# Key tiles transposed without regrouping and read by TensorE with a 16-byte step; wo loaded in three pieces

## The chip, the cores and the metric

The kernel runs on one core of a Trainium2 chip. The metric is device time in microseconds (us) of one launch; medians of all runs of a kernel are quoted. Times of the profile count from the start of the span of one profiled execution, which is one to three microseconds shorter than the time of that run.

## The reference

One decode step: attention with a sliding window over a key and value cache, a GELU layer beside it, and a sigmoid gate that mixes the two. Cut to what matters:

```python
# x: (1,1,576)  k_cache, v_cache: (1,16,32768,128)  wq: (576,4096)  wo: (4096,576)   all bf16
W = 4096                                    # the last 4096 keys of each of 16 heads
q = (x @ wq).reshape(1, 1, 32, 128)...      # 32 query heads, 2 for each key head
scores = einsum("bhqd,bhkd->bhqk", q, k) * 128 ** -0.5
a = (softmax(scores) @ v).reshape(1, 1, 4096) @ wo
b = gelu(x @ w1 + b1) @ w2 + b2
out = g * a + (1 - g) * b                   # g = sigmoid(sum(x * gate_w))
```

Keys and values are 16.8 MB each; all inputs read are 53.6 MB.

## The kernel before

The keys come from memory with the head dimension along the free axis, but TensorE must contract over it, so every key tile is transposed by VectorE in blocks of 32 by 32 words. A word is a pair of bf16 values (`bitcast(FP32)`). A key tile `k_t` holds four heads (HB = 4): partition 4k+b holds rows of head b. After the 32x32 transposes the 32 words of a block would lie in the order (k, b), the four heads interleaved. The kernel before writes them as (b, k) instead, so that the words of one head lie together.

```python
    s_ps = ps_s.tile([P, NCK * 8], FP32, name="s_ps")
    k_cuts = ((32, 32, 64), (64, 64), (64, 64), (64, 32, 32))
    for g in range(NG):                                  # 4 groups of 4 heads
        k_t = big.tile([P, NCK, Dh], BF16, name="k_t", tag="CDBA"[g])
        load(k_t, A_k_cache, g, k_cuts[g])
        for f in range(2):
            kt = kt_pool.tile([P, SL * Dh], BF16, name="kt", tag="kt")     # two buffers
            for u in range(2):
                ...
                nc.vector.transpose(
                    out=kt[:, u * half : (u + 1) * half].bitcast(FP32)
                    .rearrange("p (n b k) -> p n k b", b=HB, k=8),         # regrouped
                    in_=k_t[...].bitcast(FP32)
                    .rearrange("p (n k b) -> p n k b", b=HB, k=8))
            kv = kt[:].rearrange("p (c e b k t) -> p c e b k t", e=2, b=HB, k=8, t=2)
            for b in range(HB):
                for j in range(4):
                    nc.tensor.matmul(                                      # 128 in all
                        s_ps[:, f * 512 : (f + 1) * 512].rearrange("p (c k) -> p c k", k=8),
                        lhsT=qz[:, HB * g + b, j, :],
                        rhs=kv[:, :, j // 2, b, :, j % 2], ...)            # 4-byte step
```

Then come the softmax, the first half of w2, the value matmuls, and wo and the second half of w2 at the end. Large tiles share four buffers by tags: the w2 half takes the buffer of the third key tile ("B"), the four value tiles take C, D, A and C again, wo takes D. All large loads are issued in program order from one DMA queue, so a load that waits for its buffer holds up those behind it.

Of the kernel before, what the change touches and what calls it, by code (L numbers as in the profile page):

```python
# [8 lines left out]
FP32 = mybir.dt.float32  # L9
# [7 lines left out]
def kernel(  # L17
# [21 lines left out]
    HB = 4  # L39
# [3 lines left out]
    SL = NCK // 2  # L43
# [53 lines left out]
    for t in range(2):  # L97
        nc.vector.tensor_copy(
            out=alt[:, t : NI + 1 : 2], in_=par[:, t : t + 1].to_broadcast([P, (NI + 1) // 2])
# [6 lines left out]
    for i in range(NI):  # L106
# [3 lines left out]
            rhs=one_b[0:1, 0:1],  # L110
# [5 lines left out]
    for t in range(2):  # L116
        nc.vector.tensor_tensor(
            out=x2[:, :, t], in0=xs_ps[:], in1=alt[:, t : t + NI], op=ALU.mult
# [13 lines left out]
        out=pen[:], in0=pen[:], scalar1=1e30, scalar2=-1e30, op0=ALU.mult, op1=ALU.add  # L132
# [3 lines left out]
    for j in range(4):  # L136
# [6 lines left out]
        out=junk_row,  # L143
# [17 lines left out]
        out=omg[:], in0=g_t[:], scalar1=-1.0, scalar2=1.0, op0=ALU.mult, op1=ALU.add  # L161
# [3 lines left out]
        out=b2g[:], in0=b2_row, scalar1=omg[0:1, 0:1], scalar2=None, op0=ALU.mult  # L165
# [3 lines left out]
        out=gh[:, 0, :], in0=hi4[:], scalar1=g_t[:, 0:1], scalar2=None, op0=ALU.mult  # L169
# [21 lines left out]
    for j in range(NJ):  # L191
# [3 lines left out]
            rhs=ident[0:2, 0:2],  # L195
# [6 lines left out]
    for i in range(NI):  # L202
        for j in range(NJ):
# [3 lines left out]
                rhs=x2[:, i, :],  # L207
# [11 lines left out]
        out=poly[:],  # L219
# [20 lines left out]
    for i in range(NI):  # L240
        for j in range(Hq // 2):
# [3 lines left out]
                rhs=x2[:, i, :],  # L245
# [7 lines left out]
    for j in range(4):  # L253
# [3 lines left out]
            rhs=q_b[:],  # L257
# [3 lines left out]
    for b in range(4):  # L261
# [4 lines left out]
            out=diag[:, :, 0:512].rearrange("p h (j m) -> p h j m", m=P)[:, :, :, 0:2],  # L266
            in_=qj_ps[quad].rearrange("p j h t -> p h j t"),
# [8 lines left out]
    def load(tile_, cache, g, cuts):  # L276
        src = head_rows(cache, g)
        c0 = 0
        for n in cuts:
            nc.sync.dma_start(  # L280
                out=tile_[:, c0 : c0 + n, :].rearrange("p c d -> p (c d)"),
                in_=src[:, :, c0 * Dh : (c0 + n) * Dh],
            )
            c0 += n
# [3 lines left out]
    for g in range(NG):  # L288
# [3 lines that stand above are left out]
            kt = kt_pool.tile([P, SL * Dh], BF16, name="kt", tag="kt")  # L292
            for u in range(2):
                half = SL * Dh // 2
                c0 = f * SL + u * SL // 2
                nc.vector.transpose(  # L296
                    out=kt[:, u * half : (u + 1) * half]
                    .bitcast(FP32)
                    .rearrange("p (n b k) -> p n k b", b=HB, k=8),
                    in_=k_t[:, c0 : c0 + SL // 2, :]  # L300
                    .rearrange("p c d -> p (c d)")
                    .bitcast(FP32)
                    .rearrange("p (n k b) -> p n k b", b=HB, k=8),
                )
            kv = kt[:].rearrange("p (c e b k t) -> p c e b k t", e=2, b=HB, k=8, t=2)
            for b in range(HB):
                for j in range(4):
                    h = HB * g + b
                    nc.tensor.matmul(  # L309
                        s_ps[:, f * 512 : (f + 1) * 512].rearrange("p (c k) -> p c k", k=8),  # L310
                        lhsT=qz[:, h, j, :],
                        rhs=kv[:, :, j // 2, b, :, j % 2],
                        start=(h == 0 and j == 0),
                        stop=(h == Hkv - 1 and j == 3),
                        skip_group_check=True,
                    )
# [10 lines left out]
        out=mh4[:],  # L327
# [11 lines left out]
        out=negm[:], in0=pen[:], in1=mb_ps[:].to_broadcast([P, HB]), op=ALU.add  # L339
# [4 lines left out]
    for f in range(2):  # L344
        cs = slice(f * SL, (f + 1) * SL)
        for b in range(HB):
            nc.scalar.activation(  # L347
                out=p_t[:, cs, :, b],
                in_=s_ps[:, f * 512 : (f + 1) * 512].rearrange("p (c k) -> p c k", k=8),
# [6 lines left out]
            out=pt[:, cs, :].rearrange("p c h -> p (c h)"),  # L356
            in_=p_t[:, cs, :, :].rearrange("p c k b -> p (c k b)"),
# [6 lines left out]
    for f in range(NJ):  # L364
# [13 lines left out]
        out=rgh[:],  # L378
# [8 lines left out]
    for g in range(NG):  # L387
        v_t = big.tile([P, NCK, Dh], BF16, name="v_t", tag="CDAC"[g])
        load(v_t, A_v_cache, g, v_cuts[g])
        for c in range(NCK):  # L390
# [3 lines left out]
                rhs=pt[:, c, 8 * g : 8 * g + 8],  # L394
# [5 lines left out]
    RO = Hq * Dh // P  # L400
    wo_t = big.tile([P, RO, D], BF16, name="wo_t", tag="D")
    wo_src = A_wo.rearrange("(p r) n -> p r n", r=RO)
    for r0, r1 in ((0, 12), (12, RO)):
        nc.sync.dma_start(out=wo_t[:, r0:r1, :], in_=wo_src[:, r0:r1, :])
    for j0, j1 in ((0, 9), (9, 14), (14, 16), (16, 17), (17, 18)):
        nc.sync.dma_start(out=w2_t[:, NJ + j0 : NJ + j1, :], in_=w2_src[:, 1, j0:j1, :])
# [3 lines left out]
        out=om[:], in0=o_ps[:].to_broadcast([P, Hq, 4]), in1=rgh[:], op=ALU.mult  # L410
# [10 lines left out]
    for f in range(NJ, NF):  # L421
# [5 lines left out]
        out=out.rearrange("a b (s d) -> (a b s) d", s=2), in_=out_row[0:64:32, :]  # L427
# [31 lines left out]
```

## Time and profile before

| | before |
|---|---|
| median time | 150.57 us (3 runs, 149.56 to 151.6) |
| profiled span | 149.5 us |
| key transposes, VectorE | 16 of 3776 ns, 30.7 to 89.0 us |
| score matmuls, TensorE | 128 of 512 columns; 216 ns apart at best |
| scores end | 94.4 us |
| DMA | 53.8 MB, two holes |

The page shows the span in 40 slices of 3.7 us; a digit is a busy share in tenths (slices are counted from 0 below), PEclk is the clock granted to TensorE. These are four rows of part 2 of the page of the kernel before, and the two lines of part 4, the chain of work that ended last:

```profile
PE   0189991700768188909094949550069936361791
DVE  5990022099999999999999980406350000100001
PEclk9999999999999956999969595997555555555579
DMA  5999999999999999950089999999963899999940
...
DVE 38%; DMA 33%; PE 15%; ACT 7%; issue 5%; SPq 0%; DVEq 0%; ACTq 0%
DVE kt L296 34%; DMA wo_t<-in_A_wo_dram 14%; DMA wq_t<-in_A_wq_dram 14%; ACT p_t L347 6%; PE y_ps L178 5%; PE o_ps L391 5%; DMA w_t<-in_B_w_dram 4%; PE s_ps L309 4%; DVE pt L355 2%; DVE m L320 1%; PE q_ps L242 1%; PE t_ps L373 0%; DVE qz_flat L265 0%; DVE out_row L425 0%; PE mt_ps L322 0%
```

VectorE is busy without a gap from slice 8 to slice 23. The DMA row has a hole at slices 18 and 19 (67 to 75 us) and a dip at 29 and 30 (108 to 116 us). The chain says the same: the transposes of line 296 are its largest part.

The groups of the same page, with busy time and mean ns after the bar, and idle time before them after the second bar:

```profile
L296 DVE STREAM_TRANSPOSE kt<-k_t 128x2048 f32<-128x2048 f32 x16 | 58.3, 3776 | 0.0
L309 PE MATMUL s_ps<-kt,qz_flat 128*128 128x512 bf16 x128 | 38.6, 466 | 26.1 <-DVE kt L296 26.1
```

VectorE waits for nothing; TensorE waits 26.1 us for transposes. In the timeline of the key stage (start, length, engine) one sees the batches of 16 matmuls, and the issue of the w2 half on the DMA queue:

```profile
45.57 3.62 PE L309 MATMUL s_ps<-kt,qz_flat 128*128 128x512 bf16 x16 [2.06 <-DVE kt L296]
52.82 6.51 PE L309 MATMUL s_ps<-kt,qz_flat 128*128 128x512 bf16 x16 [3.63 <-DVE kt L296]
74.56 0.34 SPq L363 DMA_DIRECT2D w_t<-in_B_w_dram  x1
89.09 5.30 PE L309 MATMUL s_ps<-kt,qz_flat 128*128 128x512 bf16 x16 [1.95 <-DVE kt L296]
```

A batch takes 3.62 us when the clock is granted in full, which is 216 ns per matmul once the 376 ns of the last one are taken off ((3.62 - 0.376) / 15), and more when the clock is throttled (6.51 us at a mean granted clock of 0.55). The first batch (38.2 us) is an exception: it takes 5.29 us although the record has a full clock there. The Trainium skill ("TensorE: Matmul & The Clock Gate", "Back-to-back issue gap") gives 512/2.4 + 2.5 = 216 ns for a matmul of 512 columns on a warm array; the trace agrees. The section calls this the gap of an isolated matmul and puts a sustained stream at about 131 ns; no batch here averaged less than 215 ns. So with a 4-byte step TensorE reads at its full rate of one column per 0.42 ns.

### The profile page before, as it was taken

To read this page: it belongs to the slowest core of one execution; us is meant where nothing else is said; L and a number is where in the kernel's file an instruction comes from. 1 tells how busy PE (TensorE), PEld (TensorE's weight loads), DVE (VectorE), ACT (ScalarE), POOL (GpSimd) and SP (SyncE) were. 2 spreads that over 40 slices of the span, in tenths; PEclk is the share of its full clock that TensorE was granted. 3 is DMA by queue.
4 is the path that set the end of the run, shared out by engine and by line. 5 is a ranking of instruction groups with operands and counts; after the bars stand their busy time and mean duration, and the time that the engine had idled before them with its cause. 6 is when DMAs were issued, how large, how long until landed. Compare 5 with 4: busy or idle time off the path is not lost.

```text
span 149.5 us, 2460 instructions
## 1 busy us (share of the span) xinstructions
PE 85.1 (57%) x1126; PEld 53.3 (36%) x1126; DVE 78.7 (53%) x81; ACT 11.9 (8%) x21; POOL 0.7 (0%) x6
## 2 busy tenths in 40 slices
PE   0189991700768188909094949550069936361791
PEld 0187991600223022404031313230069936330450
DVE  5990022099999999999999980406350000100001
ACT  3000000010000000000000000099600000000000
POOL 1000000000000000000000000000000000000000
PEclk9999999999999956999969595997555555555579
DMA  5999999999999999950089999999963899999940
GB/s 163 428 429 420 434 431 397 421 445 434 425 421 419 421 434 425 408 237 0 0 277 427 444 438 447 438 460 421 430 298 66 377 403 428 451 437 393 404 158 0
DMA packets 4344, 53.78 MB, mean 360 GB/s; under 512 B 487, under 2 KB 748, under 8 KB 1006
## 3 DMA queue, kind: packets, MB, share of 16 engines
q1 hardware_dynamic: 4324, 53.61, 85.9%
q8 instruction: 9, 0.15, 0.4%
q10 hardware_dynamic: 10, 0.01, 0.0%
q14 instruction: 1, 0.01, 0.0%
HBM read 53.62 MB, written 0.00 MB: 359 GB/s over the span
## 4 chain that ended last, share of the span: by engine, by line
DVE 38%; DMA 33%; PE 15%; ACT 7%; issue 5%; SPq 0%; DVEq 0%; ACTq 0%
DVE kt L296 34%; DMA wo_t<-in_A_wo_dram 14%; DMA wq_t<-in_A_wq_dram 14%; ACT p_t L347 6%; PE y_ps L178 5%; PE o_ps L391 5%; DMA w_t<-in_B_w_dram 4%; PE s_ps L309 4%; DVE pt L355 2%; DVE m L320 1%; PE q_ps L242 1%; PE t_ps L373 0%; DVE qz_flat L265 0%; DVE out_row L425 0%; PE mt_ps L322 0%
## 5 line engine op out<-in xcount | busy, mean ns | idle before, releaser
L296 DVE STREAM_TRANSPOSE kt<-k_t 128x2048 f32<-128x2048 f32 x16 | 58.3, 3776 | 0.0
L309 PE MATMUL s_ps<-kt,qz_flat 128*128 128x512 bf16 x128 | 38.6, 466 | 26.1 <-DVE kt L296 26.1
L309 PEld LDWEIGHTS <-qz_flat 128*128 128x128 bf16 x128 | 14.5, 113 | 49.8 <-issue 39.9
L391 PE MATMUL o_ps<-pt,v_t 128*128 128x8 bf16 x512 | 14.3, 168 | 4.6 <-issue 4.1
L391 PEld LDWEIGHTS <-v_t 128*128 128x128 bf16 x512 | 14.2, 104 | 4.8 <-issue 4.2
L347 ACT ACTIVATE p_t<-s_ps,negm 128x512 bf16<-128x512 f32 x8 | 9.7, 1425 | 66.4 <-DVE negm L338 66.4
L178 PE MATMUL y_ps<-wo_t,ov 128*1 128x288 bf16 x64 | 8.0, 443 | 6.3 <-DMA wo_t<-in_A_wo_dram 6.3
L204 PEld LDWEIGHTS <-w_t 128*128 128x128 bf16 x162 | 10.2, 165 | 1.0 <-issue 1.0
L204 PE MATMUL h_ps<-x,w_t 128*128 128x2 bf16 x162 | 10.4, 202 | 0.0
L409 DVE TENSOR_TENSOR om<-o_ps,rgh 128x128 bf16<-128x128 f32 x1 | 0.3, 291 | 18.0 <-PE o_ps L391 18.0
L425 DVE CAST out_row<-y_ps 33x288 bf16<-33x288 f32 x1 | 0.4, 449 | 16.4 <-PE y_ps L178 16.4
L355 DVE STREAM_TRANSPOSE pt<-p_t 128x2048 bf16<-128x2048 bf16 x2 | 4.6, 2311 | 7.4 <-ACT p_t L347 7.4
L178 PEld LDWEIGHTS <-ov 128*1 128x1 bf16 x64 | 4.0, 122 | 9.9 <-issue 6.3
L373 PE MATMUL t_ps<-ls,ones 128*128 128x32 f32 x2 | 0.6, 398 | 10.8 <-DVE ls L371 10.8
L242 PE MATMUL q_ps<-x,wq_t 128*128 128x2 bf16 x144 | 4.3, 166 | 4.0 <-DMA wq_t<-in_A_wq_dram 4.0
L242 PEld LDWEIGHTS <-wq_t 128*128 128x128 bf16 x144 | 4.1, 104 | 4.2 <-DMA wq_t<-in_A_wq_dram 4.2
L178 PE MATMUL y_ps<-w_t,gt 128*1 128x288 bf16 x72 | 5.3, 289 | 0.0
L213 DVE COPY hacc<-h_ps 128x36 f32<-128x36 f32 x1 | 0.2, 195 | 9.7 <-PE h_ps L204 9.7
L107 PE MATMUL xs_ps<-one_b,rows 1*128 1x1 bf16 x9 | 0.7, 195 | 6.6 <-DVE rows L104 6.6
L373 PEld LDWEIGHTS t_ps<-ls,ones 128*128 128x128 f32 x2 | 0.5, 313 | 11.1 <-issue 11.1
L320 DVE TENSOR_REDUCE m<-s_ps 128x1 f32<-128x1024 f32 x1 | 1.2, 1225 | 5.4 <-PE s_ps L309 5.4
L201 DVE MEMSET qz_flat<- 128x4240 f32 x1 | 3.6, 3592 | 0.9 <-issue 0.9
(66 smaller groups left out, 27.6 us busy)
## 6 DMA issues: line engine op xcount, KB each, us to landing
k_t<-in_A_k_cache_dram SPq DMA_DIRECT2D x6, 2048.0 KB, 31.9
v_t<-in_A_v_cache_dram SPq DMA_DIRECT2D x3, 4096.0 KB, 24.4
w_t<-in_B_w_dram SPq DMA_DIRECT2D x3, 1728.0 KB, 10.4
k_t<-in_A_k_cache_dram SPq DMA_DIRECT2D x4, 1024.0 KB
wo_t<-in_A_wo_dram SPq DMA_DIRECT2D x1, 2880.0 KB
w_t<-in_B_w_dram SPq DMA_DIRECT2D x1, 2592.0 KB
wq_t<-in_A_wq_dram SPq DMA_DIRECT2D x1, 2048.0 KB
v_t<-in_A_v_cache_dram SPq DMA_DIRECT2D x1, 2048.0 KB
```

The lines of the kernel that those rows point to most:

```text
L107: nc.tensor.matmul(xs_ps[:, i : i + 1], lhsT=xdup[:, i : 2 * D : NI], rhs=one_b[0:1, 0:1], start=(i == 0), stop=(i == NI - 1), skip_group_ ...
L178: nc.tensor.matmul(y_ps[32 * s : 32 * s + 1, :], lhsT=vec, rhs=row[:, s * DH : (s + 1) * DH], start=start, stop=stop, skip_group_check=True,)
L201: nc.vector.memset(qz_flat[:].bitcast(FP32), 0.0)
L204: nc.tensor.matmul(h_ps[:, j:NF:NJ], lhsT=w1_t[:, i, j:FH:NJ], rhs=x2[:, i, :], start=False, stop=(i == NI - 1 and j == NJ - 1), skip_grou ...
L242: nc.tensor.matmul(q_ps[:, j : Hq : Hq // 2], lhsT=wq_t[:, i, j * Dh : (j + 1) * Dh], rhs=x2[:, i, :], start=(i == 0 and j == 0), stop=(i ...
L296: nc.vector.transpose(out=kt[:, u * half : (u + 1) * half] .bitcast(FP32) .rearrange("p (n b k) -> p n k b", b=HB, k=8), in_=k_t[:, c0 : c ...
L309: nc.tensor.matmul(s_ps[:, f * 512 : (f + 1) * 512].rearrange("p (c k) -> p c k", k=8), lhsT=qz[:, h, j, :], rhs=kv[:, :, j // 2, b, :, j ...
L320: nc.vector.reduce_max(out=m1[:], in_=s_ps[:], axis=AX.X)
L347: nc.scalar.activation(out=p_t[:, cs, :, b], in_=s_ps[:, f * 512 : (f + 1) * 512].rearrange("p (c k) -> p c k", k=8), func=ACT.Exp, bias=n ...
L355: nc.vector.transpose(out=pt[:, cs, :].rearrange("p c h -> p (c h)"), in_=p_t[:, cs, :, :].rearrange("p c k b -> p (c k b)"),)
L373: nc.tensor.matmul(t_ps[:], lhsT=ones[:], rhs=ls[:], start=True, stop=True)
L391: nc.tensor.matmul(o_ps[:, 8 * g : 8 * g + 8, 0], lhsT=v_t[:, c, :], rhs=pt[:, c, 8 * g : 8 * g + 8], start=(c == 0), stop=(c == NCK - 1),)
```

## The change

The intent: VectorE bounds the key stage, and the regrouping makes its transposes slow, since every word is written 32 bytes from the one before. So transpose plainly, let the four heads stay interleaved, and let TensorE pick every fourth key, which lies 16 bytes from the one before. In addition wo is loaded in three pieces, so that the last matmuls start in smaller batches.

```diff
                 nc.vector.transpose(
-                    out=kt[:, u * half : (u + 1) * half]
-                    .bitcast(FP32)
-                    .rearrange("p (n b k) -> p n k b", b=HB, k=8),
-                    in_=k_t[:, c0 : c0 + SL // 2, :]
-                    .rearrange("p c d -> p (c d)")
-                    .bitcast(FP32)
-                    .rearrange("p (n k b) -> p n k b", b=HB, k=8),
+                    out=kt[:, u * half : (u + 1) * half].bitcast(FP32),
+                    in_=k_t[:, c0 : c0 + SL // 2, :].rearrange("p c d -> p (c d)").bitcast(FP32),
                 )
-            kv = kt[:].rearrange("p (c e b k t) -> p c e b k t", e=2, b=HB, k=8, t=2)
+            kv = kt[:].rearrange("p (c e k b t) -> p c e k b t", e=2, b=HB, k=8, t=2)
...
-                        rhs=kv[:, :, j // 2, b, :, j % 2],
+                        rhs=kv[:, :, j // 2, :, b, j % 2],
...
-    for r0, r1 in ((0, 12), (12, RO)):
+    for r0, r1 in ((0, 12), (12, 24), (24, RO)):
```

## The prediction

> **What bounds it now.** The page puts 34% of the last chain on the key transposes and 33% on DMA. In the timeline 16 transposes run back to back from 30.7 to 89.0 us (3776 ns each, about 3.64 us start to start); the last 16 score matmuls end at 94.4. The DMA queue moves 53.8 MB at about 430 GB/s (some 125 us) and has two holes in the 40 slices: 66-76 us, where the w2 half waits for the third key tile's buffer (issued 74.6), and 109-116 us, where the last value load waits for the softmax and the first 128 value matmuls. The second follows the scores' end by a fixed path (94.4 to 110.3, 16 us).
>
> **What the change does.**
> 1. Transposes lose the regrouping, which writes every word 32 bytes from the last. The contiguous 128x2048 bf16 transpose of this trace takes 2311 ns; I take the same for fp32. VectorE: 58 to 36 us, DMA-paced (1 MiB per 2.45 us): done near 71 us if nothing blocks.
> 2. The 128 score matmuls now read one key per 16 bytes instead of four. Today's 4-byte step runs at full rate: 16 matmuls in 3.62 us at granted clock 1.0, 216 ns apart. The Trainium skill ("SBUF — State Buffer", "Door 1", on cachelines) says that SBUF has 16-byte lines and that full bandwidth needs two hits per line. This trace agrees for other reads: weight loads with a 36-byte step are 63.6 ns apart (54 in 3.43 us), contiguous ones 29.4 ns; VectorE's 128x128 reduction takes 371 ns at a 32-byte step, 266 ns at 8. No moving operand with such a step is in the trace, so its size is an estimate. Most likely half rate: about 427 ns each, 6.9 us per 16, against 4.9 us of key arrival.
> 3. wo in three pieces: the 40 matmuls (4.96 us) that start at 139.1 after the second piece become 24 earlier and 16 later; worth at most 1 us.
>
> **Critical path.** At half rate TensorE replaces VectorE as the limit of the key stage: from 35 us, 8 times 6.9, scores end near 90.5 instead of 94.4. Transposes then wait for kt. The first DMA hole shrinks (w2 issued near 67.5); the second, which counts, ends 4 us earlier. Span about 149.5 - 4 - 0.5 to 1 = 145 us.
> If strided streaming cost nothing or up to 1.5x, scores end at 76-80 us, both holes close, DMA is continuous and the time is about 133-134 us. If it costs four times (850 ns per matmul or more), the key stage takes 110 us and the whole about 200.
> Chances: half rate 0.5, cheap 0.17, about four times 0.33.
>
> **Predicted** 145.5 us, 8 in 10 within 133 to 200. Faster by over 2%: 0.62; within 2%: 0.06; slower by over 2%: 0.32.
>
> **What would show it.** The groups: transpose mean near 2.2-2.3 us; score matmuls about 430 ns apart even at clock 1.0. The waits: TensorE waits for transposes little, VectorE for kt held by matmuls much. The chain: score matmuls in place of transposes. The slices: first hole 2 us or less; second still there. Timeline: last wo batch of 16 matmuls, not 40.
>
> **What would make it wrong.** The one number I can't read: the cost of a 16-byte step on the moving side. Also: fp32 transposes slower than bf16 ones even when contiguous; a lower granted clock when TensorE is busy without gaps.

## The result, and the profile after

The changed kernel takes 202.78 us (median of 4 runs, 202.46 to 203.81) against 150.12 us (4 runs). The ratio is 1.350, with a 95% interval of 1.338 to 1.361: slower by 35%.

The same rows and lines of the page of the changed kernel (a slice is now 5.0 us; the matmul that was line 309 is line 304):

```profile
PE   0599460999999999999999999999973089446563
DVE  6920309441704406208026044000033520000000
PEclk9999999999999999999999999999999555555978
DMA  6999999999999000000999995970000007999980
...
PE 61%; DMA 27%; ACT 5%; DVE 3%; SPq 1%; issue 0%; ACTq 0%
PE s_ps L304 55%; DMA w_t<-in_B_w_dram 15%; DMA k_t<-in_A_k_cache_dram 12%; ACT p_t L342 5%; PE o_ps L386 3%; PE y_ps L178 2%; DVE kt L296 1%; DVE pt L350 1%; DVE m L315 1%; SPq L399 1%; SPq L280 0%; PE t_ps L368 0%; PE mt_ps L317 0%; PE mb_ps L329 0%; DVE out_row L420 0%
...
L304 PE MATMUL s_ps<-kt,qz_flat 128*128 128x512 bf16 x128 | 110.0, 1036 | 5.8 <-DVE kt L296 5.8
L296 DVE STREAM_TRANSPOSE kt<-k_t 128x2048 f32<-128x2048 f32 x16 | 36.2, 2293 | 55.8 <-PE s_ps L304 53.0
```

TensorE is now the row without gaps, from slice 7 to slice 28, and its score matmuls have taken the place of VectorE's transposes in the chain (55%, where those had 34%). The transposes fell from 3776 to 2293 ns, as intended, but they now wait 53.0 us for the matmuls to free kt buffers. The 128 matmuls take 110.0 us. The timeline shows their spacing in the weight loads between them, one for each matmul (the first rows of the stage, then a transpose pair and the issue of the w2 half):

```profile
35.52 110.03 PE L304 MATMUL s_ps<-kt,qz_flat 128*128 128x512 bf16 x128 [5.76 <-DVE kt L296]
36.37 0.13 PEld L304 LDWEIGHTS <-qz_flat 128*128 128x128 bf16 x1 [0.73 <-issue]
37.23 0.12 PEld L304 LDWEIGHTS <-qz_flat 128*128 128x128 bf16 x1 [0.73 <-issue]
38.08 0.12 PEld L304 LDWEIGHTS <-qz_flat 128*128 128x128 bf16 x1 [0.73 <-issue]
...
63.19 4.50 DVE L296 STREAM_TRANSPOSE kt<-k_t 128x2048 f32<-128x2048 f32 x2 [9.23 <-PE s_ps L304]
95.19 0.34 SPq L358 DMA_DIRECT2D w_t<-in_B_w_dram  x1
```

Each matmul takes 0.858 us, over the whole stage 110.03 / 128 = 0.860 us. The granted clock was 1.0 meanwhile, as a window of the stage shows (busy time and number of matmuls, granted clock, DMA):

```profile
core 0: us, PE busy (x), PEclk, DMA share, GB/s
35.50:145.00 109.50, 109.47 (x128) 1.00 0.61 255
```

So the throttle has no part in the loss. The spacing is 1.68 ns per column, four times the 0.42 ns of before. The w2 half is issued at 95.2 us instead of 74.6, because the buffer of the third key tile is freed later, so the first DMA hole grew from two slices of 3.7 us to six of 5.0 us. But that hole isn't what costs the time. The end of the scores moved from 94.4 to 145.6 us, by 51.2 us; the span grew by 51.5 us. What follows the scores takes what it took: 149.5 - 94.4 = 55.1 us before, 201.0 - 145.6 = 55.4 us after.

### The profile page after: what moved, and what is told of

Read it like the earlier page. It is cut to its first block, busy times and chain, and to the rows that moved or that the text cites. A ratio compares the mean times of both kernels' runs of the same rounds, so it can differ in the third digit from the quotient of the medians.

```text
span 201.0 us, 2461 instructions
## 1 busy us (share of the span) xinstructions
PE 158.6 (79%) x1126; PEld 55.6 (28%) x1126; DVE 56.5 (28%) x81; ACT 11.9 (6%) x21; POOL 0.7 (0%) x6
## 4 chain that ended last, share of the span: by engine, by line
PE 61%; DMA 27%; ACT 5%; DVE 3%; SPq 1%; issue 0%; ACTq 0%
PE s_ps L304 55%; DMA w_t<-in_B_w_dram 15%; DMA k_t<-in_A_k_cache_dram 12%; ACT p_t L342 5%; PE o_ps L386 3%; PE y_ps L178 2%; DVE kt L296 1%; DVE pt L350 1%; DVE m L315 1%; SPq L399 1%; SPq L280 0%; PE t_ps L368 0%; PE mt_ps L317 0%; PE mb_ps L329 0%; DVE out_row L420 0%
## 5 line engine op out<-in xcount | busy, mean ns | idle before, releaser
L304 PE MATMUL s_ps<-kt,qz_flat 128*128 128x512 bf16 x128 | 110.0, 1036 | 5.8 <-DVE kt L296 5.8
L296 DVE STREAM_TRANSPOSE kt<-k_t 128x2048 f32<-128x2048 f32 x16 | 36.2, 2293 | 55.8 <-PE s_ps L304 53.0
L304 PEld LDWEIGHTS <-qz_flat 128*128 128x128 bf16 x128 | 15.9, 124 | 98.2 <-issue 96.8
L178 PE MATMUL y_ps<-w_t,gt 128*1 128x288 bf16 x72 | 9.2, 419 | 2.0 <-DMA w_t<-in_B_w_dram 2.0
L178 PE MATMUL y_ps<-wo_t,ov 128*1 128x288 bf16 x64 | 5.8, 343 | 3.4 <-DMA wo_t<-in_A_wo_dram 3.4
L178 PEld LDWEIGHTS <-gt 128*1 128x1 bf16 x72 | 4.5, 116 | 5.5 <-issue 2.2
L178 PEld LDWEIGHTS <-ov 128*1 128x1 bf16 x64 | 3.3, 97 | 5.7 <-issue 3.5
```

Of the source, the lines that this page charges most:

```text
L178: nc.tensor.matmul(y_ps[32 * s : 32 * s + 1, :], lhsT=vec, rhs=row[:, s * DH : (s + 1) * DH], start=start, stop=stop, skip_group_check=True,)
L296: nc.vector.transpose(out=kt[:, u * half : (u + 1) * half].bitcast(FP32), in_=k_t[:, c0 : c0 + SL // 2, :].rearrange("p c d -> p (c d)").b ...
L304: nc.tensor.matmul(s_ps[:, f * 512 : (f + 1) * 512].rearrange("p (c k) -> p c k", k=8), lhsT=qz[:, h, j, :], rhs=kv[:, :, j // 2, :, b, j ...
```

## The experiments

Theory A: the whole loss is the 16-byte step of TensorE's moving operand, and its cost is a fixed time for every 16-byte line of SBUF that the reads touch, about 1.67 ns. Theory B: the step is not the cause; the plain transposes, or the order of the kt buffers between the engines, hold TensorE up. Within A the form of the cost is open: the Trainium skill ("SBUF — State Buffer", "Door 1", the paragraph on cachelines) has a threshold, two hits per line, and then full bandwidth.

Four of the kernels below (e2, e3, e5, e6) read wrong keys. The comparison with the reference doesn't tell whether the right keys were read in this problem. For the variants of which it is said below that they are right, the index map of the regrouped transposes was enumerated apart from the chip, for groups of one, two and four heads, and every value that TensorE reads was found to be the one wanted (no run shows this). For the kernel with quarter transfers (e7) the order was only reasoned out.

### wo in three pieces, alone (e1_wo3)

```diff
-    for r0, r1 in ((0, 12), (12, RO)):
+    for r0, r1 in ((0, 12), (12, 24), (24, RO)):
```

> The kernel before with wo in three pieces alone. Both theories: 0 to 1 us faster (at most the second wo batch of 40 matmuls, 4.96 us, is split into 24 and 16; the last w2 bytes land soon after). If it is slower, part of the loss after the change belongs to wo and not to the key stage.

Measured: 149.71 us against 149.56 us, ratio 1.001 (0.996 to 1.006), 6 and 11 runs. No gain can be seen. In the profile read first the last wo batch is down to 16 matmuls, 1.14 us; in the second one the last two pieces run as one batch of 40 again (4.76 us). In both the end then waits for the last pieces of w2.

### Plain transposes, 4-byte reads (e2_plain_read4)

```diff
-            kv = kt[:].rearrange("p (c e k b t) -> p c e k b t", e=2, b=HB, k=8, t=2)
+            kv = kt[:].rearrange("p (c e b k t) -> p c e b k t", e=2, b=HB, k=8, t=2)
...
-                        rhs=kv[:, :, j // 2, :, b, j % 2],
+                        rhs=kv[:, :, j // 2, b, :, j % 2],
```

(against the changed kernel)

> Plain transposes and wo in three pieces as in the changed kernel, but TensorE keeps its 4-byte step and so reads other words of the same kt buffers: results wrong on purpose. Theory A (the 16-byte step of the moving reads is the whole loss): matmuls 216 ns apart at granted clock 1.0, transposes 2.29 us, scores end near 76 us, both DMA holes closed, 133 to 136 us. Theory B (the plain transposes or the order of the kt buffers hold TensorE up): stays far above 150 us.

Measured: 135.76 us, ratio 0.909 (0.905 to 0.913). The DMA row of its page and three lines of its timeline (second profile):

```profile
DMA  4999999999999999999999998999899999999960
...
62.15 0.33 SPq L358 DMA_DIRECT2D w_t<-in_B_w_dram  x1
67.10 3.62 PE L304 MATMUL s_ps<-kt,qz_flat 128*128 128x512 bf16 x16 [1.30 <-DVE kt L296]
71.48 3.62 PE L304 MATMUL s_ps<-kt,qz_flat 128*128 128x512 bf16 x16 [0.77 <-DVE kt L296]
```

The record's class for this comparison is "unclear"; but the five runs lie between 135.59 and 137.34 us, and none of the kernel before is under 148.75 us. With nothing but the step put back, the same instructions on the same tiles take 3.62 us per batch in seven of the eight batches (5.29 us in the first, as before), the scores end at 75.1 us, and DMA has no hole. Theory B falls for the plain transposes. This is also what the idea would have given, 9%, had the 16-byte step been free; the prediction's 133 to 134 us for that case was close.

### Regrouped transposes, 16-byte reads (e3_regroup_read16)

```diff
-            kv = kt[:].rearrange("p (c e b k t) -> p c e b k t", e=2, b=HB, k=8, t=2)
+            kv = kt[:].rearrange("p (c e k b t) -> p c e k b t", e=2, b=HB, k=8, t=2)
...
-                        rhs=kv[:, :, j // 2, b, :, j % 2],
+                        rhs=kv[:, :, j // 2, :, b, j % 2],
```

(against the kernel before)

> The kernel before, transposes regrouped, but TensorE reads with a 16-byte step: results wrong on purpose. Theory A: matmuls 858 ns apart as in the changed kernel, key stage 8 x 13.7 = 110 us, total about 203 to 207 us (the first kt comes 3 us later). Theory B: near 150 us.

Measured in one run: 205.42 us. Its group of score matmuls on the page:

```profile
L309 PE MATMUL s_ps<-kt,qz_flat 128*128 128x512 bf16 x128 | 110.0, 1036 | 8.4 <-DVE kt L296 8.4
```

The group is the same as in the changed kernel to the last digit shown, 110.0 us and 1036 ns, with the slow transposes of before. Together with e2 this settles the cause: the step of the reads alone makes the loss.

### Pairs of heads: an 8-byte step (e4_step8)

```diff
-                    .rearrange("p (n b k) -> p n k b", b=HB, k=8),
+                    .rearrange("p (n a k b) -> p n k a b", a=2, k=8, b=2),
...
-            kv = kt[:].rearrange("p (c e b k t) -> p c e b k t", e=2, b=HB, k=8, t=2)
+            kv = kt[:].rearrange("p (c e a k b t) -> p c e a k b t", e=2, a=2, k=8, b=2, t=2)
...
-                        rhs=kv[:, :, j // 2, b, :, j % 2],
+                        rhs=kv[:, :, j // 2, b // 2, :, b % 2, j % 2],
```

(wo in three pieces too, here and below)

> Half of the regrouping: the transposes write pairs of heads together (two words per 16-byte line, then 64 bytes on) and TensorE reads with an 8-byte step, two hits per line; results right. Theory A1 (a fixed cost of 1.67 ns per new line on the moving side): 427 ns per matmul, 6.9 us per 16, scores end near 91 us, total about 144 to 146 us. Theory A2 (two hits per line are enough, as the Trainium skill says): 216 ns per matmul, total about 133 to 137 us if the transposes fall to 2.3 us too.

Measured: 147.95 us, ratio 0.991 (0.987 to 0.995). The groups:

```profile
L309 PE MATMUL s_ps<-kt,qz_flat 128*128 128x512 bf16 x128 | 55.5, 608 | 5.8 <-DVE kt L296 5.8
L296 DVE STREAM_TRANSPOSE kt<-k_t 128x2048 f32<-128x2048 f32 x16 | 36.2, 2294 | 14.9 <-PE s_ps L309 11.7 <-DMA k_t<-in_A_k_cache_dram 3.1
```

Two hits per line are not enough for TensorE: its matmuls take 55.5 / 128 = 0.434 us each over the stage, and within a batch they start 0.431 us apart: half rate, as theory A1 has it. For VectorE two hits are enough: with two words written per line the transposes take 2294 ns, no more than the plain ones. The same rule of the skill holds for one engine and fails for the other. The time came out 2 us above the 144 to 146 us expected although the scores ended where expected, at 90.9 us. The likely reason: the profiled run of before from which the sum was made had its last matmul batches at a lower granted clock, and ended its scores at 94.4 us, while the first profile of the kernel with wo in three pieces ended them at 92.6 us (its second one, of an execution 1.6 us longer, at 94.4 us again).

### Eight steps in one kernel (e5_steps)

```diff
+            rhs_m = [kt[:, 0 : 511 * 8 + 1 : 8], kt[:, 0 : 511 * 6 + 1 : 6], ...][2 * g + f]
...
-                        rhs=kv[:, :, j // 2, :, b, j % 2],
+                        rhs=rhs_m,
```

> Plain transposes; each of the eight batches of 16 score matmuls reads 512 bf16 values of its kt with another step: 16, 12, 24, 32, 8, 6, 2 and 4 bytes in this order; results wrong on purpose. Line theory (one new 16-byte line per 1.67 ns, or 0.417 ns per value, whichever is more): 858, 643 (384 lines), 858, 858, 429, 322 (192 lines), 216 and 216 ns per matmul at granted clock 1.0. Rival (a step of 16 bytes or more is the slow case, anything under it that hits a line twice is fast): 12 bytes 858 or 216, 6 and 8 bytes 216. Rival (cost grows with the distance): 24 and 32 bytes slower than 16.

One run. Some pairs of neighbouring rows of the timeline of weight loads, whose distance is the time of one matmul; the steps are 16, 12, 8 and 6 bytes; then one row each, from two windows of the timeline, for the batches with 2 and 4 bytes:

```profile
38.33 0.13 PEld L314 LDWEIGHTS <-qz_flat 128*128 128x128 bf16 x1 [0.77 <-issue]
39.23 0.13 PEld L314 LDWEIGHTS <-qz_flat 128*128 128x128 bf16 x1 [0.77 <-issue]
...
52.06 0.12 PEld L314 LDWEIGHTS <-qz_flat 128*128 128x128 bf16 x1 [0.55 <-issue]
52.74 0.13 PEld L314 LDWEIGHTS <-qz_flat 128*128 128x128 bf16 x1 [0.55 <-issue]
...
90.75 0.12 PEld L314 LDWEIGHTS <-qz_flat 128*128 128x128 bf16 x1 [0.33 <-issue]
91.21 0.13 PEld L314 LDWEIGHTS <-qz_flat 128*128 128x128 bf16 x1 [0.33 <-issue]
...
96.77 0.10 PEld L314 LDWEIGHTS <-qz_flat 128*128 128x128 bf16 x1 [0.24 <-issue]
97.11 0.10 PEld L314 LDWEIGHTS <-qz_flat 128*128 128x128 bf16 x1 [0.24 <-issue]
...
99.83 3.12 PEld L314 LDWEIGHTS <-qz_flat 128*128 128x128 bf16 x15 [0.24 <-issue]
...
103.07 3.46 PEld L314 LDWEIGHTS <-qz_flat 128*128 128x128 bf16 x16
```

Over a batch each (the granted clock was 1.0 throughout):

| step, bytes | lines per matmul | expected, ns | measured, ns | ns per line |
|---|---|---|---|---|
| 2 | 64 | 216 | 216 | |
| 4 | 128 | 216 | 225 | 1.76 |
| 6 | 192 | 322 | 341 | 1.78 |
| 8 | 256 | 429 | 452 | 1.77 |
| 12 | 384 | 643 | 676 | 1.76 |
| 16 | 512 | 858 | 900 | 1.76 |
| 24 | 512 | 858 | 893 | 1.74 |
| 32 | 512 | 858 | 918 | 1.79 |

Both rivals fall. There is no threshold at 16 bytes, for 6, 8 and 12 bytes lie on the same line through the number of lines; and the distance hardly matters, for 24 and 32 bytes cost what 16 do. Even the 4-byte step is on the line here: 225 ns, where the 2-byte step has 216 ns. A matmul costs the greater of 0.42 ns per column and a fixed time per line. That time is about 5% larger here, 1.76 ns, than in the changed kernel, 1.68 ns. Here each batch runs through the tile with one step of 32 bytes or less; there the reads take eight lines, skip eight, and go on, and the 128- and 256-byte steps of the next run have 1.68 ns too. Why this makes 5% was not tried further and stays open.

### Eight orders in one kernel (e6_orders)

```diff
+            rhs_m = [
+                kt[:, 0:2048].rearrange("p (l x) -> p l x", x=8)[:, :, 0:2],               # 1
+                kt[:, 0:2048].rearrange("p (l x) -> p x l", x=8)[:, 0:2, :],               # 2
+                kt[:, 0:2048].rearrange("p (o l x) -> p o x l", l=2, x=8)[:, :, 0:2, :],   # 3
+                ...                                                                        # 4 to 8
+            ][2 * g + f]
```

> Plain transposes; the eight batches read 512 values in eight orders; results wrong on purpose. 1: two neighbours of each line, then the next line. 2: the same values, but one of each line in a first pass and the other in a second. 3: two lines in turn, twice each. 4: a 128-byte step, four passes. 5: a 256-byte step, eight passes. 6: four neighbours of each line. 7: 512 neighbours, begun in the middle of a line. 8: the values of batch 6 in four passes, one of each line per pass. Line theory without memory (only the line of the last access is kept): 429, 858, 858, 858, 858, 216, 216, 858 ns per matmul. If two lines are kept, batch 3 takes 429. If lines stay for longer, batches 2 and 8 are fast. If the bank under the address matters, batches 4 and 5 are slower than 858.

One run. The spacings, with the granted clock, which fell in this run:

| batch | order | expected, ns | measured, ns | clock |
|---|---|---|---|---|
| 1 | two neighbours per line | 429 | 452 | 1.00 |
| 2 | the same values in two passes | 858 | 900 | 0.60 |
| 3 | two lines in turn, twice each | 858 or 429 | 676 | 0.50 |
| 4 | 128-byte step | 858 | 858 | 0.50 |
| 5 | 256-byte step | 858 | 860 | 0.50 |
| 6 | four neighbours per line | 216 | 426 | 0.50 |
| 7 | contiguous, begun in mid-line | 216 | 216 | 1.00 |
| 8 | batch 6 in four passes | 858 | 900 | 0.70 |

Two stretches of it as the windows show them, batches 4 and 6, with the header (busy time and number of matmuls, granted clock, DMA):

```profile
core 0: us, PE busy (x), PEclk, DMA share, GB/s
66.00:78.00 12.00, 12.00 (x15) 0.50 0.01 5
...
94.00:97.40 3.40, 3.40 (x9) 0.50 1.03 443
```

Four things follow. What counts is the order, not the set of values: batches 1 and 2 read the same values, the second twice as slowly; lines are not kept for a later pass. The larger steps are no slower, so nothing was seen of a bank under the address that would punish these steps. The time per line doesn't follow the granted clock: at 0.50 a matmul with one value per line still takes 858 ns. Batch 6 takes 426 ns because the columns themselves take 0.83 ns at half clock (the Trainium skill, "TensorE: Matmul & The Clock Gate", "Back-to-back issue gap", gives N/1.2, 427 ns, for this state; the trace agrees), so it says nothing of lines; the 4-byte step at full clock in e5 and in the kernel before does. Batch 3 fits neither expectation: 676 ns is three quarters of 900 ns, as if one of four reads found its line still there. That part is not explained.

### The rows of the keys put in TensorE's order by DMA (e7_key_quads)

If partition 8b+k of each quarter held what partition 4k+b holds now, a plain transpose would already leave the heads together. One transfer of 128 partitions in this order didn't build: its source pattern has four dimensions, and the program builder takes three. So each was cut in four:

```diff
-        load(k_t, A_k_cache, g, k_cuts[g])
+        for n in k_cuts[g]:
+            for q in (0, 2, 1, 3):
+                ksrc = ...rearrange("b (k c) d -> b k (c d)", k=8)     # 8 chunks of rows of quarter q
+                nc.sync.dma_start(out=k_t[32 * q : 32 * q + 32, kc0 : kc0 + n, :]..., in_=...)
```

> A way to have both gains: the key loads place the rows in the order in which TensorE reads (four transfers of 32 partitions in place of one of 128), so that plain transposes leave the 4-byte step; results right. If the transfers of 32 partitions keep 430 GB/s in all: as the 4-byte reads after plain transposes, 135 to 137 us. If each is limited to half of the rate: key loads take up to 78 us instead of 39, about 165 to 175 us.

Measured: 266.94 us, ratio 1.785 (1.778 to 1.792). The transposes took 2296 ns and the matmuls read with a 4-byte step, but the keys came at a quarter of the rate:

```profile
40.00:160.00 120.00, 34.28 (x96) 12.13 (x96) 24.84 (x11) 0.00 (x0) 0.00 (x0) 0.68 0.25 107
```

This is a window of 120 us of the key stage; its last two columns are the mean busy share of the 16 DMA engines, 0.25, and 107 GB/s. The packet records of this trace have four packets in flight for 87 of the 90 us from 60 to 150 us, where the key loads of the changed kernel have sixteen. That fits four of the sixteen engines at work, and the next transfers didn't fill the rest, although several had been issued. Half rate had been expected from the Trainium skill ("SBUF — State Buffer", "Door 1"), whose table has 189 GB/s for partitions 0 to 31. But the 32 partitions are not shown to be the reason: the source pattern was changed too, it now has the four heads as its outermost dimension where it had 32 chunks of rows, and four is just the number of packets in flight. No run separates the two. The idea is a miss in this form; with another order of the source's dimensions it is untested.

### Half the tiles as pairs, half regrouped (e8_mix)

VectorE's time and TensorE's time trade against each other: full regrouping costs VectorE 7.3 us per kt tile (58.3 us for eight) and TensorE 3.6 us; pairs cost 4.5 and 6.9 us. Alternating them balances the two.

```diff
         for f in range(2):
+            hb = 2 - f                               # 2: pairs, 1: fully regrouped
...
-                    .rearrange("p (n b k) -> p n k b", b=HB, k=8),
+                    .rearrange("p (n a k b) -> p n k a b", a=HB // hb, k=8, b=hb),
...
-                        rhs=kv[:, :, j // 2, b, :, j % 2],
+                        rhs=kv[:, :, j // 2, b // hb, :, b % hb, j % 2],
```

> Half of the key tiles with pairs (transposes 2.29 us, matmuls 430 ns), half fully regrouped (3.64 us, 216 ns), wo in three pieces; results right. From these terms: VectorE 8 x 5.85 us, TensorE 8 x 5.25 us, scores end near 84 us instead of 94 before and 91 with pairs throughout; the w2 half is issued near 69 us, which leaves a hole of some 4 us in the DMA queue; the second hole closes. About 140 us.

Measured: 143.3 us, ratio 0.957 (0.951 to 0.962). The scores ended at 85.9 us, two microseconds later than summed, and the hole ahead of the w2 half was some 6.5 us (1.9 slices of 3.5 us) where 4 had been summed. It beats both kernels.

### The mix, with the first value load ahead of w2 (e9_mix_v0)

```diff
+    v_0 = big.tile([P, NCK, Dh], BF16, name="v_t", tag="C")
+    load(v_0, A_v_cache, 0, v_cuts[0])
     nc.sync.dma_start(out=w2_t[:, 0:NJ, :], in_=w2_src[:, 0])
```

> The mixed kernel with the first value tile's load put ahead of the w2 half in the DMA queue: its buffer is free by 50 us, so it fills the hole of some 6.5 us (slices 18 to 20 of the mixed run) in which the queue waited for the third key tile's buffer. If that hole is all that the mixed kernel still loses against continuous DMA: 143.3 - 6.5 = about 137 us, near the 135.8 us of plain transposes with 4-byte reads. If the softmax then binds (the last value load waits for the first value matmuls): up to 140.

Measured: 140.62 us, ratio 0.938 (0.932 to 0.945), 6 and 11 runs: the fastest of the right kernels here. The DMA rows of the mix and of this kernel:

```profile
DMA  5999999999999999995089999999999999999920
```

```profile
DMA  5999999999999999999999999999917999999950
```

The hole at slices 18 to 20 is closed, and a smaller one has opened at slices 29 and 30, where the last value load waits for the softmax and the first value matmuls. So the result lies just above the upper end of what was expected, 140 us.

### Control: the same order without the mix (e10_before_v0)

The edit of e9 on the kernel before, with wo in three pieces.

> Control: the kernel before with wo in three pieces and the same change of order, no mixing. The key stage still ends near 92 to 94 us and the last value load still waits for the value matmuls behind it, so the first DMA hole moves into the second: 149 to 150 us, the same as before. If it falls below 146, the gain of the run above is the order's and not the mix's.

Measured: 147.95 us, ratio 0.985 (0.976 to 0.994). The order alone is worth about 1.5%, a little more than expected; the rest of the 6% is the mix's.

## Why the prediction was wrong

- **What bounds the kernel now: right.** VectorE in the key stage, then a path of about 55 us that follows the scores. In the changed kernel that path was 55.4 us, so the loss of 51.5 us is the key stage's alone. (It isn't fixed in all kernels: in e2, where DMA has no hole left, 58.6 us follow the scores.)
- **Transposes at 2.2 to 2.3 us: right.** 2293 ns.
- **The 16-byte step, "most likely half rate: about 427 ns each": this is the step that failed.** TensorE did become the limit, through the 16-byte lines, so the path was right; the size was off by a factor of two: 858 ns, and 110 us for the key stage where eight times 6.9 us had been summed. The prediction took the cost as a factor on the engine's rate, from a threshold of two hits per line and from other reads that slowed by a factor of about two or less. The runs show a fixed time per line, 1.68 to 1.79 ns, the same at full and at half clock. With four bf16 values per line that is 0.42 to 0.45 ns per value, so the 4-byte step of the kernel before lies just at the edge of free, and every hit per line that is given up costs in full: 427 ns expected at two hits (431 measured), 858 ns at one.
- **The trace of before held a better estimate.** That matmuls 216 ns apart read four values per line bounds the time per line from above by 216 / 128 = 1.69 ns. VectorE's regrouped writes, one word per line, take 3776 / 2048 = 1.84 ns each. An estimate of some 1.7 ns for a line, times 512 lines, would have been about 870 ns. That VectorE and TensorE meet the same limit in SBUF is only argued here from the likeness of the numbers, and one number speaks against a single limit for all reads: the weight loads with a 36-byte step, which touch a new line for each of their 128 columns, start 62 ns apart, 0.48 ns per line. So the time per line holds for the moving operand, and the weight loads on which the prediction leaned could not give its size.
- **TensorE in VectorE's place, transposes waiting for kt: right in kind.** VectorE waited 53.0 us for matmuls. But the first DMA hole grew where the prediction had it shrink, as the w2 half was issued at 95.2 us and not at 67.5.
- **wo in three pieces, at most 1 us: right.** Ratio 1.001 (0.996 to 1.006): no gain seen.
- **The branch with four times the cost: right in its parts.** "The key stage takes 110 us and the whole about 200" is what came, 110.0 us and 202.78 us. It was given a chance of 0.33. The range ended at 200 because that sum was of the profiled span (201.0 us came), while the time of a run is one to three microseconds longer, and the range had no margin above it. It was the second branch by weight and not the forecast.

## What to carry to other kernels

For a strided moving operand of TensorE, count the 16-byte lines of SBUF that one matmul touches: it takes the greater of 0.42 ns per column and about 1.7 ns per line (1.68 to 1.79 ns in these runs). So bf16 was free, or nearly so (216 to 225 ns), up to a 4-byte step only. When one engine must scatter so that another can gather, price both in time per line and let the two share the work: in this kernel half the tiles with an 8-byte step, half with a 4-byte step, gave 4%, and 6% with the loads put in a better order, where moving the whole cost to TensorE lost 35%.

## What the Trainium skill lacked or had wrong

- "SBUF — State Buffer" ("Door 1", on cachelines) and "Advanced Engine Details and Errata" ("SBUF Cachelines") say that two hits per line absorb the latency. For VectorE's transposes that holds: 2294 ns with two words written per line, 2293 ns plain, 3776 ns with one. For TensorE's moving operand it doesn't: it needs four bf16 values per line (216 to 225 ns); two cost 431 ns, one costs 858 ns.
- No page gives the penalty a size for TensorE's moving reads. The runs show about 1.68 ns per new line (1.74 to 1.79 ns where a batch runs through the tile with one step of 4 to 32 bytes), unchanged at a granted clock of 0.50.
